# Expert-gate blocks stored whole by two transfers from two half buffers to a padded DRAM layout

## The chip, the cores and the metric

One core of one Trainium2 chip runs the whole program. The metric is the device time of one execution in microseconds (us), as the median of several runs. The engines are TensorE (PE, matmuls; PEld are its weight loads), VectorE (DVE), ScalarE (ACT), GpSimd (POOL) and SyncE (SP, whose queue issues all the DMA transfers here).

## The reference

A sequence of 2,048 tokens with 512 features passes four layers, two pairs of a Fourier layer (A) and a mixture of 256 small experts with 32 heads (B), each with a layer norm ahead and a residual:

```python
a = einsum("bsd,ed->bse", x, dft_hid_re);  b = einsum("bsd,ed->bse", x, dft_hid_im)
y = einsum("ts,bse->bte", dft_seq_re, a) - einsum("ts,bse->bte", dft_seq_im, b)   # A

q = einsum("nd,dhc->nhc", xf, w_q)                     # B: two halves of 128
s1 = einsum("nhd,ed->nhe", q[..., :dk], k1); s2 = einsum("nhd,ed->nhe", q[..., dk:], k2)
i1, i2 = top-2 of the 16 scores s1, of the 16 scores s2
cand = t1[..., :, None] + t2[..., None, :]             # 4 candidates, experts i1 * 16 + i2
top_s, top_e = the best 2 of the 4;  g = softmax(top_s)
act = gelu(einsum("nd,nhkd->nhk", xf, u[top_e]))
out = einsum("nhk,nhk,nhkd->nd", g, act, v[top_e])
```

Since there are only 256 experts, B can be computed densely: for each token a 16 x 16 matrix holds the sum over the heads of the gates g at (i1, i2); it is multiplied by gelu(x u^T), 256 values a token, and the product by v.

## The kernel before

**Tiles and stages.** The tokens form 16 tiles of 128. For each of the two layer pairs, units of 256 tokens (the last 256 tokens as two units of 128) pass through: the sequence DFT (`seq_unit`, L519: its matrix is streamed from DRAM in pieces of 256 KB, each split into a high part `ch` by ACT at L459 and a low part `cl` by DVE at L463; the sums are in PSUM tiles `acc`), then, for each tile (`token_tile`), the hidden DFT (L659), layer norm, a transpose of the normed rows (on PE at L747, or, for most tiles, by DVE at L715 with a store L719 and a reload L728 through DRAM, cast at L735 and L738), the scores (L777, L781), evacuated by ACT to `sc` (L786), and x u^T (L808). DVE then finds the top two of 16 by trees of maxima and comparisons (L861 to L916); L861 of the second rank is the last reader of `sc`. The results, as small numbers `q`, are transposed (L989) and evacuated (`qt`, L993).

**The blocks.** With `qt`, DVE makes one-hot masks of 16 x 16 x 4 (L1012, weighted at L1018) in four `lr` buffers of 2 KB a partition. 32 matmuls (L1028) multiply them. Since each treats four tokens at once, its result is a 64 x 64 block of which only the 4 diagonal parts (16 x 16 each, both of one token) are wanted: partition (j, e, t), free (g, t', f), wanted where t = t'. Two PSUM banks hold them; ACT evacuates them, one bank at a time (L1038), into `gs`. Four transfers (L1058), one for each t, take the diagonal parts out of every fourth partition in runs of 64 B to the DRAM tile `gdr`, and two transfers (L1066) bring them back in runs of 64 B, token by partition, as `gt`. DVE multiplies `gt` into the activation (L1069). The product is transposed on PE (L1100) and multiplied by v (L1119, L1123); L1134 adds the row, L1139 or L1144 stores it. For 13 tiles of the second layer pair this last part is put off: they turn the product on DVE (L1076), store it (L1091), and at the very end `off` loads and multiplies it (L591, evacuated at L597, added at L600, stored at L601) while PE waits for the last tile.

**Buffers.** `sc` has one buffer, which serves the scores of a tile and, later, `gs` of a tile. `lr` has four, for the masks and for the rows turned at L715. The last tile (`fine`) uses other memory: the masks lie in `ch` and `cl` buffers, `gs` in the tile `pth`, `gt` in a `raw` buffer.

**The order.** Every operation is put down as an `op` with an engine, an estimated time, what it comes after, a priority, the buffers it takes (`Hold`) and gives back, and, for a transfer, a `lag` until it has landed (at most eight in flight). `Plan.run` is a list scheduler over these estimates, and the program is written out in the order of its start times, so that each engine's queue is fixed by them. `behind` orders an operation behind another one's issue alone. Where the plan sees PE idle for over 1 us after the last sequence DFT, filler matmuls are put in (L1205), one for each 0.23 us of the gap less 0.4 us.

Of the kernel before, what the change touches and what calls it, by code (L numbers as in the profile page):

```python
# [8 lines left out]
F32 = mybir.dt.float32  # L9
# [7 lines left out]
P = 128  # L17
# [7 lines left out]
SP = 1  # L25
# [3 lines left out]
E = 16  # L29
# [20 lines left out]


LATE = 13
WARY = 0.8
FILL0 = 10
FIRST = 4
# [23 lines left out]
class Plan:  # L79
# [10 lines left out]
    def op(self, engine, us, fn, after=(), take=(), last=(), prio=(0, 0), lag=0.0, behind=(), shy=0.0):  # L90
        o = Op(len(self.ops), engine, us, fn, [a for a in after if a is not None], list(take), list(last), prio, lag,
               list(behind), shy)
        for h in o.last:
            h.users += 1
        self.ops.append(o)
        return o
# [67 lines left out]
def act(n):  # L164
    return 0.09 + n / 1.2e3
# [7 lines left out]
def spectral_peer_kernel(ctx: ExitStack, tc, x_in, cseq, ctile, dhid, wq, k1t, k2t, ut, vm, out):  # L173
    nc = tc.nc
# [4 lines left out]
    dram = ctx.enter_context(tc.tile_pool(name="dram", bufs=1, space=bass.MemoryType.DRAM))  # L179
# [3 lines left out]
    BUFS = {"acc": 4, "bank": 4, "raw": 4, "c": 3, "p": 1, "row": 4, "wr": 5, "wp": 2,  # L183
            "tok": 3, "sc": 1, "eq": 1, "act": 3, "q": 2, "top": 1, "qt": 1, "lr": 4, "gt": 1, "pp": 1, "gdr": 2, "xdr": 2, "late": 3, "ev": 3, "bn": 1}
    plan = Plan(BUFS)


    xh = [const.tile([P, D], F32R, name=m, bufs=b) for m, b in (("xh", LATE), ("xg", NT - LATE)) for _ in range(b)]
    xl = [const.tile([P, D], F32R, name=m, bufs=b) for m, b in (("xl", LATE), ("xm", NT - LATE)) for _ in range(b)]
    dh = const.tile([P, 2, KD, D], F32R, name="dh")  # L190
# [38 lines left out]
    def work(shape, dtype, name, pool=None):  # L229
        return work_pool().tile(shape, dtype, name=name, bufs=BUFS[pool or name])  # L230
# [7 lines left out]
    op = plan.op  # L238
# [365 lines left out]
    last = {}  # L604
# [3 lines left out]
    def token_tile(layer, n, i, t0, at):  # L608

        prio = (0, layer, at if at < len(units) - 1 else -1 - layer, i)  # L610
        late = (0, layer, at, i, 1)
        fine = prio[:3] == FINAL
# [3 lines left out]
        t = {}  # L616
# [31 lines left out]
        for cs in wide:  # L648
            hb, nc_ = Hold("bank"), cs.stop - cs.start
            for z, (k, ms) in enumerate(steps):  # L650
                def f(z=z, k=k, ms=ms, cs=cs):
# [4 lines left out]
                    for c in range(2):  # L656
# [7 lines left out]
                       take=[hb] if z == 0 else [], behind=[a_row],  # L664
                       last=[phold[layer, n]] if z == len(steps) - 1 else [], prio=prio)
# [103 lines left out]
        for hf in range(2):  # L769
# [22 lines left out]
            if fine:  # L792
                for z, k in enumerate(ks):
                    a_pe = op("PE", 2 * (k.stop - k.start) * MM512, lambda f=f_pch, hf=hf, k=k: f(hf, k), [a_th[z], a_pe],
                              take=[] if z else [hb], prio=prio)
# [211 lines left out]
        for hf in range(2):  # L1007
# [10 lines left out]
                nc.vector.tensor_mul(t["m", hf, 1], t["m", hf, 1], row_of(2, hf))  # L1018

            made.append(op("DVE", dve(1024, 2), f_w, [a], last=[hqt] if hf else [], prio=soon))  # L1020
        hgs, hbs = Hold("p" if fine else "sc"), [Hold("bank") for _ in range(2)]

        def f_blocks(hfs=(0, 1)):
            for hf in hfs:
# [6 lines left out]
        def f_gs(hf):  # L1031
            def f():
                if hf == 0 and fine:
                    gs = apool.tile([P, KD, 2, T], F32R, name="pth").rearrange("p k c t -> p (k c t)")[:, :N * 4].bitcast(F32)
                    t["gs"] = gs.rearrange("p (g t e) -> p g t e", t=4, e=E)
                elif hf == 0:
                    t["gs"] = work([P, 16, 4, E], F32, "sc")
                nc.scalar.activation(t["gs"][:, 8 * hf:8 * hf + 8], t["pg", hf].rearrange("p g e t -> p g t e"),  # L1038
                                     AF.Copy, scale=0.5 / GSCALE)
            return f  # L1040

        if fine:
            pe = [op("PE", 16 * MMG + 0.15, lambda hf=hf: f_blocks((hf,)), [made[hf]], take=hbs[hf:hf + 1],
                     last=hls[2 * hf:2 * hf + 1], prio=prio) for hf in range(2)]
        else:
            pe = [op("PE", 32 * MMG + 0.3, f_blocks, made, take=hbs, last=hls, prio=prio)] * 2
        evac = []
        for hf in range(2):
            evac.append(op("ACT", act(512), f_gs(hf), [pe[hf]] + evac, take=[] if hf else [hgs], last=hbs[hf:hf + 1], prio=prio))


        hd, hgt = Hold("gdr"), Hold("raw" if fine else "gt")
        moves = []
        for k in range(4):
            def f_out(k=k):
                if k == 0:
                    t["gdr"] = dram.tile([2, E, 4, 16, E], F32, name="gdr", bufs=BUFS["gdr"])
                nc.sync.dma_start(t["gdr"][:, :, k].rearrange("j e g f -> (j e) g f"), t["gs"][k::4, :, k, :])  # L1058
            moves.append(op("SP", 0.3, f_out, evac[1:], behind=moves[:1], take=[hd] if k == 0 else [], last=[hgs], prio=prio,
                            lag=2.4))  # L1060
        back = []
        for j in range(2):
            def f_in(j=j):
                if j == 0:
                    t["gt"] = piece((E, E)) if fine else work([P, E, E], F32, "gt")
                nc.sync.dma_start(t["gt"][j * 64:(j + 1) * 64], t["gdr"][j].rearrange("e t g f -> (t g) e f"))  # L1066
            back.append(op("SP", 0.4, f_in, moves, behind=back, take=[hgt] if j == 0 else [], last=[hd], prio=prio, lag=3.5,
                           shy=0.0 if fine else 0.5))
        a = op("DVE", dve(N), lambda: nc.vector.tensor_mul(t["act"], t["act"], t["gt"].rearrange("p e f -> p (e f)")),  # L1069
               back + [a_act], last=[] if deferred else [hgt], prio=prio)  # L1070
# [64 lines left out]
        if layer:  # L1135
            if at == len(units) - 1:
                for o in stores[-2:]:
                    o.behind.extend(back)
            stores.append(op("SP", load(256), lambda: nc.sync.dma_start(out[i * P:(i + 1) * P, :], t["row"]), [a],  # L1139
                             last=[hrow], prio=prio, lag=2.3))  # L1140
# [4 lines left out]
                       last=[] if keep else [hrow], prio=prio, lag=2.3)  # L1145
# [113 lines left out]
```

## Time and profile before

| | us |
|---|---|
| median of 3 runs (lowest, highest) | 1251.66 (1251.53, 1252.41) |
| profiled execution, whole time | 1250.42 |
| its span, first to last instruction | 1248.7 |
| PE, DVE, ACT busy | 1226.5, 1009.6, 483.2 |
| store of the blocks `gdr<-sc`: transfers, KB each, issue to landing | 124, 32, 2.2 |
| way back `gt<-gdr`: transfers, KB each, issue to landing | 62, 64, 2.8 |
| bytes moved by DMA | 148.19 MB |

The profile is one execution. Times in it count from the first instruction. An engine executes its queue in order, so an instruction that waits holds up all behind it. A line of the waits names the waiting engine, tile and source line, then what it waited for. A matmul's busy time overlaps that of the next one, so a busy PE is not yet a PE at its peak; an idle one has surely lost time. "SPq" rows are issues of transfers; the number with them is the time of the issue, and the transfer lands later.

### The profile page before, as it was taken

The numbers are of one execution on the slowest core, as the hardware profiler recorded it, in microseconds if no ns is written. First come the engines' busy times: TensorE is split into PE (matmuls) and PEld (weight loads), VectorE is DVE, ScalarE is ACT, GpSimd is POOL, SyncE is SP. The second block draws the span as 40 slices with busy tenths as digits, with TensorE's granted clock in tenths as the row PEclk, the third lists the DMA queues.
The fourth block names the chain that finished last, engine by engine and source line by source line (L and its number), as shares of the span: only waits on it lengthen the run. The fifth ranks groups of instructions, "written<-read, shape, count | busy, mean of one in ns | idle before, by whom it ended". The sixth has DMA issues, their size and how long they took to land.

```text
span 1248.7 us, 20707 instructions
## 1 busy us (share of the span) xinstructions
PE 1226.5 (98%) x7576; PEld 1015.0 (81%) x7576; DVE 1009.6 (81%) x2290; ACT 483.2 (39%) x994; POOL 44.5 (4%) x71
## 2 busy tenths in 40 slices
PE   9999999999999999999999999999999999999997
PEld 6877778777887888899878888777888888888985
DVE  8899997988988876869877458969595877969797
ACT  7522244333333333433563233333333333333543
POOL 2000000000000000000000000000000000000000
PEclk9999999999999999999999999999999999999999
DMA  7866551343434244341556232443526343353554
GB/s 239 263 197 223 179 159 35 85 89 93 99 92 105 67 100 111 76 119 58 129 135 153 93 104 54 122 101 90 139 76 144 85 110 85 102 118 94 127 169 127
DMA packets 317766, 148.19 MB, mean 119 GB/s; under 512 B 221920, under 2 KB 287968, under 8 KB 317664
## 3 DMA queue, kind: packets, MB, share of 16 engines
q1 hardware_dynamic: 317664, 146.87, 44.3%
q8 instruction: 59, 0.97, 0.3%
q14 instruction: 43, 0.35, 0.1%
HBM read 120.86 MB, written 25.95 MB: 118 GB/s over the span
## 4 chain that ended last, share of the span: by engine, by line
PE 64%; DVE 20%; issue 6%; DMA 5%; ACT 2%; SPq 2%; POOL 1%; POOLq 0%; DVEq 0%; ACTq 0%
PE acc L519 36%; PE bank L659 9%; PE bank L777 6%; PE bank L781 3%; DVE cl L463 2%; PE bank L808 2%; DVE eq L861 2%; DVE w L385 1%; DMA raw<-x2d 1%; PE bank L519 1%; DVE lr L1012 1%; PE bank L393 1%; DVE tmp L867 1%; DVE eq L885 1%; DMA gdr<-sc 1%
## 5 line engine op out<-in xcount | busy, mean ns | idle before, releaser
L519 PE MATMUL acc<-ch,xh 128*128 128x512 f32 (+1 forms) x868 | 328.7, 379 | 1.7 <-DVE ptl L548 1.7
L519 PE MATMUL acc<-cl,xh 128*128 128x512 f32 (+1 forms) x868 | 321.9, 371 | 0.0
L519 PE MATMUL acc<-ch,xl 128*128 128x512 f32 (+1 forms) x868 | 321.8, 371 | 0.0
L459 ACT CAST ch<-raw 128x512 fp32r<-128x512 f32 x256 | 158.5, 620 | 277.5 <-PE acc L519 235.3
L463 DVE TENSOR_TENSOR cl<-raw,ch 128x512 fp32r<-128x512 f32 x256 | 175.1, 686 | 49.1 <-ACT ch L459 38.4
L519 PEld LDWEIGHTS acc<-ch,xh 128*128 128x128 f32 x868 | 163.7, 189 | 29.3 <-issue 1.8
L519 PEld LDWEIGHTS acc<-cl,xh 128*128 128x128 f32 x868 | 163.6, 188 | 28.8
L519 PEld LDWEIGHTS acc<-ch,xl 128*128 128x128 f32 x868 | 163.8, 189 | 25.2
L777 PE MATMUL bank<-wh,tok 128*128 128x512 f32 x256 | 100.3, 392 | 2.4 <-ACT tok L735 2.4
L659 PE MATMUL bank<-dh,pth 128*128 128x512 f32 (+1 forms) x264 | 102.4, 390 | 0.2
L659 PE MATMUL bank<-dl,pth 128*128 128x512 f32 (+1 forms) x264 | 100.6, 383 | 0.0
L777 PE MATMUL bank<-wl,tok 128*128 128x512 f32 x256 | 99.7, 390 | 0.0
L867 DVE TENSOR_TENSOR tmp<-sc 128x512 f32<-128x512 f32 (+1 forms) x66 | 44.3, 671 | 66.9 <-ACT sc L786 66.5
L1012 DVE TENSOR_TENSOR lr<-iota,qt 128x1024 f16<-128x1024 f16 x124 | 80.5, 683 | 21.6 <-ACT qt L993 21.6
L659 PE MATMUL bank<-dh,ptl 128*128 128x512 f32 (+1 forms) x264 | 95.6, 384 | 0.0
L786 ACT COPY sc<-bank 128x512 f32<-128x512 f32 x64 | 37.1, 587 | 127.8 <-PE bank L781 83.3
L261 POOL TENSOR_TENSOR stats<-stats,half 128x1 f32<-128x1 f32 x64 | 43.2, 681 | 1160.7 <-DVE stats L258 1081.3
L861 DVE TENSOR_TENSOR eq<-sc,val 128x1024 f16<-128x1024 f32 (+1 forms) x66 | 78.6, 1190 | 1.6
L519 PE MATMUL acc<-ch,xg 128*128 128x512 f32 (+1 forms) x204 | 77.1, 378 | 0.0
L519 PE MATMUL acc<-cl,xg 128*128 128x512 f32 (+1 forms) x204 | 75.8, 372 | 0.1
L519 PE MATMUL acc<-ch,xm 128*128 128x512 f32 (+1 forms) x204 | 75.6, 371 | 0.0
L781 PE MATMUL bank<-wh,tok 128*128 128x512 f32 x256 | 68.6, 390 | 1.1 <-DVE tok L738 1.1
(166 smaller groups left out, 2045.2 us busy)
## 6 DMA issues: line engine op xcount, KB each, us to landing
raw<-in_cseq SPq DMA_DIRECT2D x224, 256.0 KB, 2.9
wr<-in_wq SPq DMA_DIRECT2D x32, 512.0 KB, 3.9
raw<-in_ctile SPq DMA_DIRECT2D x32, 256.0 KB, 2.9
xdr<-lr SPq DMA_DIRECT2D x25, 256.0 KB, 2.3
tok<-xdr SPq DMA_DIRECT2D x100, 64.0 KB, 2.6
wr<-in_x SPq DMA_DIRECT2D x16, 256.0 KB, 3.6
row<-in_x SPq DMA_DIRECT2D x16, 256.0 KB, 3.4
x2d<-row SPq DMA_DIRECT2D x16, 256.0 KB, 2.2
```

Source lines behind the costliest of these rows:

```text
L261: nc.gpsimd.tensor_tensor(st[:, 1:2], st[:, 1:2], half, op=ALU.pow)
L459: nc.scalar.copy(t[1], t[0])
L463: nc.vector.tensor_sub(t[2], t[0], as32(t[1]))
L519: nc.tensor.matmul(target(d), w[s][:, d * P:(d + 1) * P], moving(s % per, part), start=(s == 0 and k == 0 and d % blocks == 0), stop=(s == ...
L659: nc.tensor.matmul(t["y", cs.start], w[:, k, c, t0:t0 + P], r[:, c, k, cs], start=(z == 0 and c == 0 and m == 0), stop=(z == len(steps) - ...
L777: nc.tensor.matmul(t["pc", hf], t["th"][:, k, :], r[:, k, hf], start=(k == 0 and r is wh), stop=False)
L781: nc.tensor.matmul(t["pc", hf], t["tl"][:, k, :], wh[:, k, hf], start=False, stop=(k == KD - 1))
L786: nc.scalar.copy(t["sc"][:, :, hf, :], t["pc", hf].rearrange("p h e -> p e h"))
L808: nc.tensor.matmul(t["xu"], w[:, k, :], r[:, k, :], start=(m == 0), stop=(m == 3 * KD - 1))
L861: nc.vector.tensor_tensor(t["eq"][:, :, cols], flat("sc")[:, :, cols], val(rank_, cols), op=ALU.is_equal)
L867: nc.vector.tensor_max(t["tmp"][:, :, cols], flat("sc")[:, :8, cols], flat("sc")[:, 8:, cols])
L1012: nc.vector.tensor_tensor(t["m", hf, r], io2, row_of(r, hf), op=ALU.is_equal)
```

## The change

The two halves of the evacuated blocks become two tiles of their own: two `lr` buffers, or, for the last tile, the two halves of the same `pth` memory. Each half is stored whole, diagonal and rest, by one transfer from 128 partitions with runs of 256 B, right after its own evacuation. In DRAM, a block row of 64 numbers has a place of `STEP` = 80, and a partition's row starts every `ROW` = 16 x 80 - 16 numbers. By that offset of 16 the diagonal parts of the four token positions lie at equal steps, and each of the two transfers back can take them with one step of 80 over 64 partitions and one of 4 x `ROW` over the 16 values of e. The plan gets new estimates: 0.6 us and a lag of 2.7 for a store (0.3 and 2.4 before, for each of four), 0.6 and 3.2 for a transfer back (0.4 and 3.5).

```diff
+STEP = 5 * E
+ROW = 16 * STEP - E
...
-        hgs, hbs = Hold("p" if fine else "sc"), [Hold("bank") for _ in range(2)]
+        hgs, hbs = [Hold("p")] * 2 if fine else [Hold("lr"), Hold("lr")], [Hold("bank") for _ in range(2)]
...
-                    t["gs"] = gs.rearrange("p (g t e) -> p g t e", t=4, e=E)
-                elif hf == 0:
-                    t["gs"] = work([P, 16, 4, E], F32, "sc")
-                nc.scalar.activation(t["gs"][:, 8 * hf:8 * hf + 8], t["pg", hf].rearrange("p g e t -> p g t e"),
+                    gs = gs.rearrange("p (g t e) -> p g t e", t=4, e=E)
+                    t["gs", 0], t["gs", 1] = gs[:, :8], gs[:, 8:]
+                elif not fine:
+                    t["gs", hf] = work([P, 8, 4, E], F32, "lr")
+                nc.scalar.activation(t["gs", hf], t["pg", hf].rearrange("p g e t -> p g t e"),
                                      AF.Copy, scale=0.5 / GSCALE)
...
-            evac.append(op("ACT", act(512), f_gs(hf), [pe[hf]] + evac, take=[] if hf else [hgs], last=hbs[hf:hf + 1], prio=prio))
+            evac.append(op("ACT", act(512), f_gs(hf), [pe[hf]] + evac, take=[] if fine and hf else hgs[hf:hf + 1], last=hbs[hf:hf + 1], prio=prio))
...
-        for k in range(4):
-            def f_out(k=k):
-                if k == 0:
-                    t["gdr"] = dram.tile([2, E, 4, 16, E], F32, name="gdr", bufs=BUFS["gdr"])
-                nc.sync.dma_start(t["gdr"][:, :, k].rearrange("j e g f -> (j e) g f"), t["gs"][k::4, :, k, :])
-            moves.append(op("SP", 0.3, f_out, evac[1:], behind=moves[:1], take=[hd] if k == 0 else [], last=[hgs], prio=prio,
-                            lag=2.4))
+        for hf in range(2):
+            def f_out(hf=hf):
+                if hf == 0:
+                    t["gdr"] = dram.tile([2, E, 4, ROW], F32, name="gdr", bufs=BUFS["gdr"])
+                d = t["gdr"][0]
+                d = bass.AP(d.tensor, d.offset + hf * 8 * STEP, [[ROW, P], [STEP, 8], [1, 4 * E]])
+                nc.sync.dma_start(d, t["gs", hf].rearrange("p g t e -> p g (t e)"))
+            moves.append(op("SP", 0.6, f_out, evac[hf:hf + 1], behind=moves[-1:], take=[] if hf else [hd], last=[hgs[hf]], prio=prio,
+                            lag=2.7))
...
-                nc.sync.dma_start(t["gt"][j * 64:(j + 1) * 64], t["gdr"][j].rearrange("e t g f -> (t g) e f"))
-            back.append(op("SP", 0.4, f_in, moves, behind=back, take=[hgt] if j == 0 else [], last=[hd], prio=prio, lag=3.5,
+                d = t["gdr"][j]
+                d = bass.AP(d.tensor, d.offset, [[STEP, 64], [4 * ROW, E], [1, E]])
+                nc.sync.dma_start(t["gt"][j * 64:(j + 1) * 64], d)
+            back.append(op("SP", 0.6, f_in, moves, behind=back, take=[hgt] if j == 0 else [], last=[hd], prio=prio, lag=3.2,
                            shy=0.0 if fine else 0.5))
```

## The prediction

> **What bounds the kernel now.** I read the page first, then the busy time by stages (the windows view), then who waited for whom, the DMA issues, and last the timeline at the places that these named. The page's first lines:
>
> ```profile
> span 1248.7 us, 20707 instructions
> PE 1226.5 (98%) x7576; PEld 1015.0 (81%) x7576; DVE 1009.6 (81%) x2290; ACT 483.2 (39%) x994; POOL 44.5 (4%) x71
> ```
>
> TensorE (PE) is busy for 1226.5 of 1248.7 us, so all that any edit outside TensorE can win is in the 22.2 us of idle PE. The profiled execution took 1250.42 us, 1.72 more than its span; the median of the runs is 1251.66, 1.24 above that execution. I make the sum against 1250.42 and carry the difference over to the median. Where the idle PE lies (columns: stretch, its length, then busy time and instructions of each engine, clock, DMA share, GB/s):
>
> ```profile
> 228.00:600.00 372.00, 369.36 (x2225) 309.29 (x2224) 308.95 (x758) 138.34 (x299) 14.67 (x23) 1.00 0.38 93
> 600.00:690.00 90.00, 85.92 (x547) 72.67 (x547) 68.11 (x155) 44.12 (x86) 3.55 (x4) 1.00 0.52 135
> 690.00:1203.00 513.00, 508.84 (x2890) 424.41 (x2889) 386.10 (x897) 192.51 (x403) 8.61 (x16) 1.00 0.43 107
> 1203.00:1248.70 45.70, 37.78 (x232) 29.11 (x230) 35.76 (x100) 16.80 (x38) 0.92 (x1) 0.99 0.45 121
> ```
>
> Between the first gather (about 228 us) and the last unit's end, PE idles for 2.64 + 4.08 + 4.16 = 10.9 us; in the tail, where the last tile's latency counts, for 7.9 us. The rest lies ahead of the first gather, where the change has nothing to alter. Which waits have to do with the blocks that the change touches (columns: total us, times, longest):
>
> ```profile
> ACT sc L1038 <- DVE eq L861: 43.0, 17, 7.5
> ...
> ACT sc L786 <- DVE eq L861: 24.0, 4, 7.4
> ...
> DVE lr L1012 <- ACT qt L993: 21.6, 13, 3.3
> ACT sc L786 <- DMA gdr<-sc: 20.5, 6, 7.3
> ...
> DVE act L1069 <- DMA gt<-gdr: 9.0, 10, 1.7
> ```
>
> There is a single buffer named sc, and it holds in turn the scores of a tile (L786) and the evacuated blocks of a tile (L1038). So an evacuation waits until VectorE has read the next tile's scores to the end (43.0 us), and a score copy waits until the four transfers of the blocks have landed (20.5 us). These are waits of ScalarE, which is 39% busy; they cost time only where PE then waits. PE's own list:
>
> ```profile
> PE bank L777 <- ACT tok L735: 2.4, 2, 1.3
> ...
> PE bank L989 <- DVE q L956: 1.8, 3, 0.7
> ...
> PE bank L1100 <- DVE act L1069: 1.5, 1, 1.5
> PE bank L781 <- DVE tok L738: 1.1, 1, 1.1
> ...
> PE bank L808 <- ACT sc L1038: 0.8, 1, 0.8
> ```
>
> **The change part by part. Buffers.** The blocks go to two lr buffers instead of sc. The L1038 wait of 43.0 us and the L786 wait of 20.5 us lose their cause. What that is worth on PE is read at the places where the chain from the one to the other can be followed. At 304 us it is direct: the evacuation waits 7.50 us for L861, and PE's L808, which needs one of the PSUM banks that the evacuation frees, idles for 0.76 us.
>
> ```profile
> 304.55 0.60 ACT L1038 ACTIVATE sc<-bank 128x512 f32<-128x512 f32 x1 [7.50 <-DVE eq L861]
> ...
> 305.20 0.39 PE L808 MATMUL bank<-uh,tok 128*128 128x256 f32 x1 [0.76 <-ACT sc L1038]
> ```
>
> At 817 us the four stores go out, ScalarE stands still for 7.32 us until they have landed, everything behind L786 on its queue (the casts of the next DFT pieces, L735) comes late, and PE idles 1.09 us at L781:
>
> ```profile
> 817.35 2.73 SPq L1058 DMA_DIRECT2D gdr<-sc  x4
> ...
> 823.68 1.08 ACT L786 COPY sc<-bank 128x512 f32<-128x512 f32 x2 [7.32 <-DMA gdr<-sc]
> ...
> 833.84 0.50 PE L781 MATMUL bank<-wh,tok 128*128 128x512 f32 x1 [1.09 <-DVE tok L738]
> ```
>
> **The SP queue.** Four store issues become two. At 1091 us the xdr store (L719), whose data DVE had turned from 1091.12 on, stands behind the four issues until 1094.13; its reload and cast come late by as much, and PE idles 1.15 us at L777:
>
> ```profile
> 1091.12 1.43 DVE L715 STREAM_TRANSPOSE lr<-tok 128x512 f32<-128x512 f32 x2 [0.17 <-ACT tok L272]
> 1091.39 2.65 SPq L1058 DMA_DIRECT2D gdr<-sc  x4
> 1094.13 1.05 SPq L719 DMA_DIRECT2D xdr<-lr  x2
> ...
> 1103.28 0.50 PE L777 MATMUL bank<-wh,tok 128*128 128x512 f32 x1 [1.15 <-ACT tok L735]
> ```
>
> What an issue of the new kind costs (128 partitions of 8 runs) no row shows; the neighbours are the old store (32 partitions of 16 runs) and the xdr store (128 partitions of one run):
>
> ```profile
> L1058 SPq DMA_DIRECT2D gdr<-sc x124: 577/631/1760, 228.4 to 1226.6; - x124
> ...
> L719 SPq DMA_DIRECT2D xdr<-lr x25: 319/376/624, 271.8 to 1094.8; - x25
> ```
>
> I take 0.63 us, the nearer in runs (512 of them; the new one has 1,024), with 0.38 and 1.26 (twice 0.63, by runs) as ends. Two issues then hold the queue 1.26 us in place of 2.5; at the far end nothing is saved.
>
> **The transfers.** Median landings (columns: instances, KB each, us from issue to landing):
>
> ```profile
> wr<-in_wq SPq DMA_DIRECT2D x32, 512.0 KB, 3.9
> ...
> xdr<-lr SPq DMA_DIRECT2D x25, 256.0 KB, 2.3
> ...
> gdr<-sc SPq DMA_DIRECT2D x124, 32.0 KB, 2.2
> gt<-gdr SPq DMA_DIRECT2D x62, 64.0 KB, 2.8
> ```
>
> A new store moves 128 x 8 x 64 x 4 B = 256 KB in runs of 256 B. It is no faster than the 256 KB store in runs of 2 KB (2.3), and I bound it above by the 512 KB load (3.9). I take 2.9, since the 1,024 runs are as many as gt<-gdr has (2.8). Both kinds come to 2,048 runs a tile, so the packet count stays, while the bytes grow by 384 KB a tile, 12.6 MB in all; at a DMA share of 0.38 to 0.52 they find room. The Trainium skill, "DMA: Bandwidth & Descriptors", Specifications, says that transfers reach line rate only from 512 B on and that shorter ones cost a read-modify-write; the new runs, with 256 B, stay below. By that rule alone the store would lie nearer to 3.9 than to 2.3; the 2.2 us of the 64-byte store shows no such penalty at 32 KB, and no row here shows one at 256 KB. The way back keeps its 1,024 runs of 64 B a transfer. Only their spacing in DRAM changes (320 B and 20 KB steps); I leave it at 2.8, with the same ends, 2.3 and 3.9.
>
> **The end of the span** is where the latency of a gather counts in full. The last tile's:
>
> ```profile
> 1229.99 0.60 ACT L1038 ACTIVATE pth<-bank 128x512 f32<-128x512 f32 x1 [2.01 <-PE bank L1028]
> ...
> 1231.31 0.60 ACT L1038 ACTIVATE pth<-bank 128x512 f32<-128x512 f32 x1 [0.72 <-PE bank L1028]
> ...
> 1231.93 2.63 SPq L1058 DMA_DIRECT2D gdr<-pth  x4
> ...
> 1236.36 1.38 SPq L1066 DMA_DIRECT2D raw<-gdr  x2
> ...
> 1238.86 2.66 PE L1205 MATMUL acc<-dh 128*128 128x512 f32 x11
> ...
> 1240.28 0.42 DVE L1069 TENSOR_TENSOR act<-act,raw 128x256 f32<-128x256 f32 x1
> 1241.35 0.38 PE L1100 MATMUL bank<-identf,act 128*128 128x128 f32 x2
> ```
>
> Now the way back starts 1236.36 - 1231.91 = 4.45 us after the second evacuation. Afterwards the first half leaves at 1230.6, hidden by the second evacuation, and the second half needs about 3.0 us, 2.9 and 0.1 until the next issue starts: 1.4 us earlier (2.0 by the low end, 0.4 by the high one). But the multiply (L1069) is done at 1240.70, and the transpose behind it (L1100) starts at 1241.35 only, since eleven filler matmuls (L1205) stand ahead of it on PE: about 0.65 us that are lost already. Their number comes from the plan's gap. The plan's own costs take the gather from 4 x 0.3 + 2.4 + 2 x 0.4 + 3.5 = 7.9 us to 0.6 + 2.7 + 2 x 0.6 + 3.2 = 7.7 after the evacuation: 0.2 us, about one filler (2.66 us for eleven, 0.24 each). So most of the 1.4 us ends in front of the fillers, unless the PE work ahead of them also moves up: the gather of the tile before it no longer waits for sc. I take 0.5 us, nearer to the one filler, with ends 0.2 and 1.4.
>
> **The sum.** The three PE waits followed above, 0.76 + 1.09 + 1.15 = 3.0 us, and 0.5 us at the end: 3.5 us. Everything else is put at nothing: DVE and ACT run the same instructions, and PE's 1.5 + 1.8 us at L1100 and L989 I leave, since I could not follow them to the gather. 1250.42 - 3.5 = 1246.9 for a profiled execution, 1251.66 - 3.5 = **1248.2** for the median. With all five rows of PE's list gone (7.6 us) and 1.4 at the end it would be 9.0 less, 1242.7; with only 2.0 of the 3.5 had, 1249.7.
>
> **The rivals. Nothing that counts moves.** The order of every instruction is made by a list scheduler from cost estimates, and with other holds and costs it is made anew from about 228 us on. The named waits go, but PE's waits are short, scattered misjudgements of the plan, and another order has its own. For it speaks that 96.5 us of waits in the four rows with sc, gdr or gt (43.0 + 24.0 + 20.5 + 9.0) correspond to at most 7.6 us of idle PE; against it, that the most frequent cause (one buffer, two uses) is taken away rather than moved. Then only 0.5 us at the end remains: 1251.2. It reaches from 1249.2, where the forecast begins, to 1252.7, with one more wait of the size of the longest in PE's list, 1.5 us.
>
> **The new stores are slow.** If a store lands after 3.9 us, the gather is 0.4 us shorter and not 1.4, the last tile gives 0.2 us, and the SP part of the sum (1.15) shrinks to nothing, since the issues of the way back then hold that queue until the landing; 0.76 + 1.09 + 0.2 = 2.05 us remain: 1249.6. The line-rate rule above would be its reason, and a measured landing decides.
>
> **Slower: the masks wait for lr.** The four lr buffers now hold the masks (L1012 takes all four), the turned rows (L715) and, from evacuation to landing, the two halves. If the next masks or turned rows come before the halves have landed, VectorE waits in its queue, and the cl halves of the DFT pieces (L463) behind it, on which PE lives. Today L1012 waits for nothing but its own qt (21.6 us), which speaks against it, and L715 shows that a claim can follow the stores closely, which speaks for it. The price: 96.5 us of waits gave up to 7.6 us of idle PE, 0.08 us for each. If each of the 31 tiles ahead of the last waits 3 us for lr, that is 93 x 0.08 = 7.3 us, against 3.5 won: 3.8 slower, 1255.5. It turns the sign from 3.5 / 0.08 = 44 us of waits on, 1.4 us a tile.
>
> **How the numbers follow.** The forecast gets 0.50, nothing moves 0.29, slow stores 0.07, lr 0.14. A measurement of this kernel tells changes from about 0.2%, 2.5 us. The forecast lies beyond that (1249.2 and below), the next two within it, lr above: faster 0.50, same 0.36, slower 0.14. The forecast's own range is 1242.7 to 1249.2. The whole range goes from 1243.0 (nearly all waits gone) over the two middle cases up to 1253.5, where lr has begun to cost: it leaves out most of lr's 0.14 and a little at the low end.
>
> **What would show it.** Stores gdr<-lr, 62 of them, 256 KB each, landing at 2.3 to 3.3 us with an issue of about 0.63; some 12.6 MB more, the packets under 512 B hardly changed in number; no wait of the evacuation on eq L861 and none of L786 on a landing; PE idle between 228 and 1203 us down from 10.9 to 7 or 8; the last way back within 3.3 us of the last evacuation. I am wrong if PE's idle there stays at 10 or more, if a DVE wait on gdr<-lr stands among the first rows, or if the fillers ahead of the last L1100 grow by what the gather saves.

## The result

The changed kernel takes 1238.62 us (median of 4 runs, 1237.93 to 1239.08) against 1251.6 us in 4 runs of the kernel before beside them: a ratio of 0.9902, 95% interval 0.989 to 0.9914. The prediction had the sign right and the size wrong: 3.5 us were forecast, 13.0 came, and 1238.62 lies below the low end of the range. Its profiled execution took 1238.99 us. The first lines of its page:

```profile
span 1237.2 us, 20626 instructions
PE 1223.0 (99%) x7572; PEld 1015.8 (82%) x7572; DVE 1007.8 (81%) x2290; ACT 484.9 (39%) x994; POOL 45.3 (4%) x71
```

The span is 11.5 us shorter. (The medians lie 13.0 apart: the profiled execution of before was 1.2 us faster than its kernel's median, that of the changed kernel 0.4 slower.) Idle PE falls from 22.2 to 14.2 us, which is 8.0 of it. The other 3.5 us come out of PE's *busy* time: four fillers fewer (4 x 0.23 = 0.9 us), and some 2.6 us by which the same matmuls follow each other more closely.

The same stretches in the windows view:

```profile
228.00:600.00 372.00, 370.50 (x2231) 311.56 (x2230) 309.86 (x758) 139.65 (x299) 16.01 (x23) 1.00 0.43 107
600.00:690.00 90.00, 89.59 (x591) 77.55 (x590) 70.17 (x160) 47.44 (x89) 3.55 (x5) 1.00 0.57 150
690.00:1203.00 513.00, 512.01 (x2896) 427.38 (x2895) 391.39 (x914) 194.10 (x409) 8.98 (x16) 1.00 0.47 119
1203.00:1237.20 34.20, 26.49 (x178) 20.06 (x176) 26.12 (x76) 12.52 (x27) 0.00 (x0) 1.00 0.52 146
```

PE's idle time in the first three is 1.50 + 0.41 + 0.99 = 2.9 us, where it was 10.9. At the boundary of the layer pairs (600 to 690 us) 591 matmuls fit in the 90 us that held 547.

The best yardstick is the end of the last matmul of the sequence DFT, behind which only the tail is left. From the timeline of PE, before and then after:

```profile
1197.36 0.28 PE L519 MATMUL acc<-cl,xg 128*128 128x256 f32 x1
```

```profile
1186.55 0.28 PE L521 MATMUL acc<-cl,xg 128*128 128x256 f32 x1
```

It ends at 1197.64 and at 1186.83: **10.8 us** of the 11.5 were won ahead of it. The tail behind it went from 51.1 to 50.4, **0.7 us**. In the rest of this document "DFT end" is this point and "tail" what follows it.

The waits that answer to those shown of before (total us, times, longest):

```profile
ACT sc L788 <- DVE eq L863: 30.1, 7, 5.6
...
ACT lr L1041 <- PE bank L1030: 19.8, 14, 4.7
...
DVE lr L1014 <- ACT qt L995: 12.2, 10, 3.1
```

The evacuation (now L1041) waits for its own matmuls and no longer for VectorE's comparisons; its 43.0 us are gone, and so are the 20.5 us of the score copy behind the landings. The score copy's wait for the comparisons, the first row, stays (24.0 before). The masks (L1014) wait for `qt` alone, as before, and no row for `lr` buffers stands near the top. The tile that waited 7.50 us at 304 us goes like this now (timeline):

```profile
286.49 0.69 PE L1030 MATMUL bank<-lr 128*64 128x64 f16 x32
...
287.86 1.06 ACT L1041 ACTIVATE lr<-bank 128x512 f32<-128x512 f32 x2
...
288.47 1.01 SPq L1063 DMA_DIRECT2D gdr<-lr  x2
...
292.37 1.33 SPq L1073 DMA_DIRECT2D gt<-gdr  x2
...
298.18 0.42 DVE L1076 TENSOR_TENSOR act<-act,gt 128x256 f32<-128x256 f32 x1
```

The blocks are evacuated 1.4 us after their first matmul starts; in the kernel before, whose matmuls of this tile started at 292.64, that took 11.9 us, to 304.55. Over all 32 tiles the mean time from the last of these matmuls to the first evacuation fell from 6.0 to 0.0 us, and to the multiply from 17.0 to 10.75. The gather itself, from the second evacuation to the last landing of the way back, hardly changed: 8.95 to 8.07 us. So the gather was not made fast; it was let start.

The transfers (instances, KB each, us to landing), and then the issues of `gdr` (shortest, median, longest in ns):

```profile
gdr<-lr SPq DMA_DIRECT2D x62, 256.0 KB, 3.7
...
gt<-gdr SPq DMA_DIRECT2D x62, 64.0 KB, 3.0
...
gdr<-pth SPq DMA_DIRECT2D x2, 256.0 KB, 2.6
```

```profile
L1063 SPq DMA_DIRECT2D gdr<-lr x62: 366/424/1599, 221.9 to 1207.4; - x62
...
L1073 SPq DMA_DIRECT2D gt<-gdr x62: 579/640/1373, 226.7 to 1211.4; - x62
```

A store lands 0.8 us later than I took, and holds the queue for 0.42 us where I took 0.63.

### The profile page after: what moved, and what is told of

Same layout as the page of the kernel before. It is cut to its first block, busy times and chain, and to the rows that moved or that the text cites. A ratio compares the mean times of both kernels' runs of the same rounds, so it can differ in the third digit from the quotient of the medians.

```text
span 1237.2 us, 20626 instructions
## 1 busy us (share of the span) xinstructions
PE 1223.0 (99%) x7572; PEld 1015.8 (82%) x7572; DVE 1007.8 (81%) x2290; ACT 484.9 (39%) x994; POOL 45.3 (4%) x71
## 2 busy tenths in 40 slices
DMA packets 316742, 160.76 MB, mean 130 GB/s; under 512 B 220897, under 2 KB 286945, under 8 KB 316641
## 5 line engine op out<-in xcount | busy, mean ns | idle before, releaser
L1014 DVE TENSOR_TENSOR lr<-iota,qt 128x1024 f16<-128x1024 f16 x124 | 80.8, 684 | 12.3 <-ACT qt L995 12.2
```

The source lines that it names most:

```text
L1014: nc.vector.tensor_tensor(t["m", hf, r], io2, row_of(r, hf), op=ALU.is_equal)
```

## The experiments

All of them run the kernel's whole work; they differ in where the blocks lie, how they are stored, and what the plan is told. The recorded texts name three theories. A: the gain comes from the blocks leaving `sc`. B: it comes from two transfers in place of four. C: luck, the new order simply has fewer bad places. From tied_plan on, A has two forms, called D and W here. D: the single `sc` buffer costs through the *plan*: since blocks and scores can't both hold it, the scheduler puts one tile's evacuation and the next one's scores behind each other, and PE's work with them. W: the real waits on the chip cost (evacuations behind the comparisons, score copies behind the landings). Each ratio is to runs of the kernel before taken beside it. Results (DFT end, idle PE from 228 us to the DFT end, and evacuation, the mean us from the last blocks matmul to the first evacuation, are from each kernel's one profiled execution; the first half can leave before the second half's matmuls end, hence values at or below 0):

| kernel | blocks in | stores a tile | ratio (95%) | DFT end | idle | evac. |
|---|---|---|---|---|---|---|
| before | sc | 4 of 32 KB | 1 | 1197.6 | 10.9 | 6.0 |
| changed | lr | 2 of 256 KB | .9902 (.9890–.9914) | 1186.8 | 2.7 | 0.0 |
| halves_in_sc | sc | 2 of 256 KB | .9988 (.9978–.9998) | 1194.4 | 7.4 | 5.8 |
| halves_in_sc_b | sc | 2 of 256 KB | .9971 (.9955–.9988) | 1195.0 | 9.5 | 7.4 |
| halves_in_sc_c | sc | 2 of 256 KB | .9991 (.9982–1.0001) | 1195.4 | 8.0 | 5.6 |
| tied_plan | lr, plan sc | 2 of 256 KB | .9930 (.9910–.9950) | 1190.4 | 4.8 | 4.4 |
| tied_plan_b | lr, plan sc | 2 of 256 KB | .9973 (.9963–.9984) | 1193.3 | 7.4 | 6.1 |
| tied_plan_c | lr, plan sc | 2 of 256 KB | .9997 (.9987–1.0008) | 1195.5 | 9.0 | 4.0 |
| evac_waits_eq | lr, plan sc | 2 of 256 KB | .9955 (.9940–.9970) | 1189.5 | 4.8 | 5.7 |
| other_costs | lr | 2 of 256 KB | .9885 (.9869–.9901) | 1184.5 | 1.1 | 0.05 |
| other_costs_b | lr | 2 of 256 KB | .9903 (.9888–.9918) | 1185.6 | 1.9 | 0.1 |
| measured_costs | lr | 2 of 256 KB | .9917 (.9902–.9932) | 1184.2 | 0.7 | 0.05 |
| early_told | lr | 2 of 256 KB | 1.0209 (1.0192–1.0226) | 1220.2 | 23.3 | 0.0 |
| four_small | one lr of 4 KB | 4 of 32 KB | .9924 (.9909–.9938) | 1189.7 | 3.2 | 0.0 |
| two_whole | one lr of 4 KB | 2 of 256 KB | .9905 (.9888–.9921) | 1187.0 | 3.0 | −0.1 |
| eight_small | lr | 8 of 16 KB | .9962 (.9948–.9976) | 1192.8 | 6.6 | 0.1 |
| eight_whole | lr | 8 of 64 KB | .9899 (.9883–.9916) | 1186.6 | 2.3 | 0.1 |
| eight_small_told | lr | 8 of 16 KB | 1.0024 (1.0013–1.0035) | 1196.5 | 8.7 | −0.1 |
| banks_late | lr | 2 of 256 KB | .9905 (.9888–.9921) | 1188.2 | 2.7 | 0.0 |
| scores_late | lr | 2 of 256 KB | .9988 (.9978–.9997) | 1192.0 | 5.8 | −0.1 |

Single runs of one kernel lie up to some us apart (15 runs of the kernel before: 1249.45 to 1254.21), so a us more or less in the last three columns says nothing.

**One part alone: whole stores, blocks still in sc.** The edit of halves_in_sc to the changed kernel:

```diff
-        hgs, hbs = [Hold("p")] * 2 if fine else [Hold("lr"), Hold("lr")], [Hold("bank") for _ in range(2)]
+        hgs, hbs = [Hold("p" if fine else "sc")] * 2, [Hold("bank") for _ in range(2)]
...
+                    gs = work([P, 16, 4, E], F32, "sc")
+                    t["gs", 0], t["gs", 1] = gs[:, :8], gs[:, 8:]
```

The plan's estimate for a store is 0.7 us and a lag of 2.8 here, since with 0.6 and 2.7 the scheduler finds no way through.

> The changed kernel with the two evacuated halves put back into the single sc buffer (one tile of 4 KB a partition); the two whole stores, the padded layout and the transfers back stay. The plan's estimate of a store is 0.7 us and a lag of 2.8, since the plan has no solution with 0.6 and 2.7. Theory A (the gain comes from the blocks leaving the sc buffer, so that the evacuation follows its matmuls at once): 1248 to 1253 us, evacuations wait again for eq, some 6 us after the matmuls. Rival B (the gain comes from two transfers in place of four): 1238 to 1242 us. Rival C (the new order is luckier): anywhere, since the order is new again.

Ratio 0.9988 (1249.4 us), as A said: about a tenth of the gain; the granted clock has a share in that, told below. Its waits show why, and its window at the boundary that nothing improved there:

```profile
ACT sc L1042 <- DVE eq L863: 41.9, 16, 5.6
...
ACT sc L788 <- DMA gdr<-sc: 21.0, 9, 6.2
```

```profile
600.00:690.00 90.00, 86.24 (x541) 73.00 (x541) 70.45 (x160) 46.19 (x88) 3.80 (x5) 0.98 0.56 151
```

The two waits for `sc` are as long as before the change (43.0 and 20.5).

**The other part alone: two halves in lr, small stores.** eight_small is the kernel before with the two `lr` halves and, for each half, the four strided stores of before at half their size:

```diff
-        hgs, hbs = Hold("p" if fine else "sc"), [Hold("bank") for _ in range(2)]
+        hgs, hbs = [Hold("p")] * 2 if fine else [Hold("lr"), Hold("lr")], [Hold("bank") for _ in range(2)]
...
-        for k in range(4):
+        for hf, k in itertools.product(range(2), range(4)):
...
-                nc.sync.dma_start(t["gdr"][:, :, k].rearrange("j e g f -> (j e) g f"), t["gs"][k::4, :, k, :])
+                nc.sync.dma_start(t["gdr"][:, :, k, 8 * hf:8 * hf + 8].rearrange("j e g f -> (j e) g f"), t["gs", hf][k::4, :, k, :])
```

> The kernel before with the blocks in two lr halves, each stored as soon as it is evacuated, but with stores of the diagonal parts as before, 64 B a run, now four for each half, eight in all of 16 KB; layout and way back as before. Theory A: 1238 to 1243 us although SP issues twice as many stores as before, evacuations right behind the matmuls. Rival B: 1251 us or more, by up to 2.5 us a tile of issues on the queue. Rival C: anywhere.

Ratio 0.9962 (1246.4 us), outside both ranges: more than whole stores in `sc` gave, but not the whole. Whether the number of the issues or their form holds it back is the question for eight_whole below.

**Only the plan keeps the tie.** tied_plan is the changed kernel in all that runs; only the scheduler is told that an evacuation still takes `sc` and that the stores give it back (estimates as in halves_in_sc; parts of the two changed lines):

```diff
+        htie = Hold("sc")
...
-take=[] if fine and hf else hgs[hf:hf + 1],
+take=([] if fine and hf else hgs[hf:hf + 1]) + ([] if fine or hf else [htie]),
...
-last=[hgs[hf]],
+last=[hgs[hf]] + ([] if fine else [htie]),
```

> The changed kernel (store estimate 0.7 and 2.8) with its two lr halves, but the plan alone also lets the first half take sc and gives it back when both stores have landed, as before: the order is made as if the blocks lay in sc, and on the chip no buffer makes anyone wait for it. Theory A in the form that the plan's order is what costs (late evacuations hold PSUM banks, later scores): 1247 to 1253 us. Theory A in the form that the unplanned waits on the chip cost: 1239 to 1243 us. Rival B: 1239 to 1243 us.

other_costs is the changed kernel without the tie, with the same two estimates (0.7 and 2.8), another order by luck alone:

> The changed kernel with the plan's estimate of a store at 0.7 us and a lag of 2.8 in place of 0.6 and 2.7, nothing else: the control for the runs that need these estimates, and a new order of the same work. Theory A and rival B: 1237 to 1241 us. Rival C: 1243 us or more is as likely as not.

The tie in the plan turns 0.9885 into 0.9930, so D has a part. But 1242.6 us lies in the range set for W, not in that for D: tied_plan is still 0.6% faster than halves_in_sc. The two traces list the same instructions in the same order on every engine, and so do those of the two pairs that follow; in each pair the real buffer alone differs. So the pair was repeated in other orders, first with 0.6 and 3.0 for a store and 0.4 and 3.5 for the way back.

> halves_in_sc once more with other estimates in the plan (store 0.6 and 3.0, back 0.4 and 3.5), so another order of the same work. Theory A: 1247 to 1252 us again, evacuations some 6 us after the matmuls. If the order's luck decides (rival C), anything from 1237 to 1254.

> tied_plan once more with the other estimates (store 0.6 and 3.0, back 0.4 and 3.5), the partner of halves_in_sc_b (ratio 0.9971) and other_costs_b (0.9903): buffers free on the chip, order as if they were not. If the three steps found with the first estimates hold for a second order: about half way, 1240 to 1245 us. If the order's luck made them: anywhere.

> The changed kernel with those estimates (store 0.6 and 3.0, back 0.4 and 3.5): a third order of the changed kernel. Theory A: 1235 to 1241 us. Rival C: 1243 us or more would be as likely as not.

Here the times with and without the real buffer are level (0.9971 and 0.9973; tied_plan_b was not half way), and freeing the plan is worth 0.7% (0.9903, in its range). A third pair, with 1.2 and 2.4 for a store:

> halves_in_sc with a third set of estimates (store 1.2 and 2.4, back 0.4 and 3.5): 1245 to 1252 us as the other two (ratios 0.9988 and 0.9971).

> tied_plan with the same third set, against halves_in_sc_c: the same order, no buffer that makes anyone wait on the chip. If the real waits cost some 7 us, as with the first set: 1239 to 1243 us. If they cost nothing, as with the second set: within 2 us of halves_in_sc_c.

Level again (0.9991 and 0.9997). The changed kernel with these estimates and no tie was not run. In tied_plan_c no evacuation waits for a comparison and no score copy for a landing; the evacuation's own row, and PE's boundary stretch, which is still like the one before the change:

```profile
ACT lr L1042 <- PE bank L1031: 10.0, 6, 5.2
```

```profile
600.00:690.00 90.00, 86.33 (x551) 74.19 (x550) 66.48 (x152) 43.66 (x83) 4.31 (x4) 0.98 0.56 148
```

So in two of three orders, with the real waits of the blocks on `sc` gone, an order made for a shared buffer is as slow as one that has the waits. C is out as the main cause: the changed kernel in four orders (0.9885, 0.9902, 0.9903, 0.9917) stays within 0.3%, far from the 1.0% to be explained, and the tied ones lie at 0.9930 to 0.9997 (only the first one's interval reaches theirs). The 0.6% of the first pair was left; evac_waits_eq was to settle it: tied_plan with the real wait put back, by a tiny copy into an `sc` buffer ahead of the evacuation:

```diff
+                    if hf == 0:
+                        gate = work([P, 16, 4, E], F32, "sc")
+                        nc.scalar.copy(gate[:, 0, 0, :1], half)
```

> The run tied_plan (same order, same buffers) with one thing put back on the chip: ahead of a tile's first evacuation ScalarE writes one number per partition into a tile of the sc buffer, so the evacuation waits again until VectorE has read the scores in sc to the end; no store reads sc, so no score copy waits for a landing. One instruction of about 0.2 us more a tile. If the real wait of the evacuation is what cost the difference between halves_in_sc (ratio 0.9988) and tied_plan (0.993): 1248 to 1250 us. If the wait of the score copies for the landing was: 1242 to 1244 us.

0.9955 lies between the two ranges and settles little. The tiny copy waits as long as the real evacuations of halves_in_sc (41.9 us):

```profile
ACT sc L1044 <- DVE eq L863: 39.1, 16, 5.6
```

So the wait for the comparisons is not the whole 0.6%, and as the intervals of 0.9955 and 0.9930 overlap, it may be none of it. Halves_in_sc_b and halves_in_sc_c wait for the comparisons as long (42.5 and 49.6 us), but for the landings only half as long as the 21.0 us of halves_in_sc:

```profile
ACT sc L788 <- DMA gdr<-sc: 10.6, 5, 5.6
```

```profile
ACT sc L788 <- DMA gdr<-sc: 10.5, 6, 4.2
```

That points at the landings as what the first pair paid for; no run tried them alone.

**The granted clock** has a share in these ratios. In tied_plan's trace TensorE's clock stands at half once for 3.4 us, right behind 3.4 us in which PE was idle for 1.5 (windows of 3.4 us, columns as in the stretches above):

```profile
662.60:666.00 3.40, 1.91 (x38) 1.34 (x38) 3.30 (x7) 1.80 (x4) 0.00 (x0) 1.00 0.69 227
666.00:669.40 3.40, 3.40 (x10) 2.62 (x9) 0.12 (x1) 0.16 (x1) 0.00 (x0) 0.50 1.00 225
```

There a 128 x 512 matmul starts every 0.427 us, elsewhere every 0.227, so one such stretch costs about 1.7 us, in PE's busy time. Between 228 us and the DFT end the kernel before and the changed one have none; halves_in_sc and tied_plan_c have one, halves_in_sc_c and tied_plan_b two, early_told five, and ahead of each (or of two in a row) PE stood idle for 1.4 us or more of 3.4. As an estimate, take (1 - granted clock) x span off every run (one reading of 0.945 and one of 0.949 left out, since their runs are not slower by as much) and compare medians with the kernel before treated alike: halves_in_sc and its two repeats gain 3.8, 3.7 and 5.0 us, the tied plans 8.3, 5.5 and 5.0, evac_waits_eq 7.7, and other_costs, other_costs_b and measured_costs 14.0, 11.9 and 12.3. So the tie in the plan costs some 6 us by this estimate, and the real buffer 4.5, 1.8 and 0 on top; halves_in_sc and its repeats have about a third of the gain, of which the lost clock takes most away in the first and the third. Since each of these stretches follows idle time of PE, I count them with what the order costs, but that is a reading, not a test.

**The form of the transfers.** eight_whole has the plan, and so the order, of eight_small, and stores whole rows, 32 partitions at a time:

```diff
-        for hf in range(2):
+        for hf, k in itertools.product(range(2), range(4)):
...
-                d = bass.AP(d.tensor, d.offset + hf * 8 * STEP, [[ROW, P], [STEP, 8], [1, 4 * E]])
-                nc.sync.dma_start(d, t["gs", hf].rearrange("p g t e -> p g (t e)"))
+                d = bass.AP(d.tensor, d.offset + hf * 8 * STEP + 32 * k * ROW, [[ROW, 32], [STEP, 8], [1, 4 * E]])
+                nc.sync.dma_start(d, t["gs", hf][32 * k:32 * k + 32].rearrange("p g t e -> p g (t e)"))
```

> The changed kernel with each half stored by four transfers of 32 partitions (64 KB, still whole, 256 B a run) in place of one; eight issues a tile, with the estimates and so the order of eight_small (ratio 0.9962). If the eight issues on the SP queue are what keeps eight_small from the changed kernel's time: 1245 to 1248 us, as eight_small or a little slower, gather about 10 us. If the form of the runs is: 1237 to 1241 us.

0.9899 against 0.9962, as good as two stores. In the same order the issues of eight_small and then of eight_whole:

```profile
L1059 SPq DMA_DIRECT2D gdr<-lr x248: 576/612/1402, 221.0 to 1217.3; - x124
```

```profile
L1063 SPq DMA_DIRECT2D gdr<-lr x248: 303/450/1818, 221.7 to 1209.0; - x124
```

A store of rows taken from every fourth partition holds the queue 0.61 us, one of 32 whole neighbours 0.45, though it moves four times the bytes. The gather is 10.35 us against 8.84, and what stands behind these issues comes late. Waits of eight_small, then of eight_whole:

```profile
ACT tok L735 <- DMA tok<-xdr: 21.5, 12, 3.5
DVE act L1070 <- DMA gt<-gdr: 14.9, 16, 3.6
```

```profile
ACT tok L737 <- DMA tok<-xdr: 5.3, 4, 2.6
...
DVE act L1076 <- DMA gt<-gdr: 1.8, 2, 1.3
```

Is the cost that the plan does not know the length? eight_small_told tells it (0.6 us for each store and each transfer back):

> eight_small (ratio 0.9962, gather some 1.5 us longer than in eight_whole and than the plan believes) with the plan told of the length: 0.6 us for each of the eight stores and each transfer back in place of 0.3 and 0.4. The gather itself stays as long. If multiplies that come later than planned are what cost eight_small its 8 us against eight_whole: 1238 to 1241 us. If the length of the gather or the 0.61 us of each issue on the queue is: 1244 to 1248 us.

No: 1.0024 (1253.0 us, above both ranges), though the wait for `xdr` halves (to 10.2 us). That reading fell. Whether the queue's time or the longer gather costs is not separated.

**Small stores with the buffer freed, four of them.** four_small is the kernel before with its four stores, layout and estimates, its blocks in `lr`. For that, `lr` becomes two buffers of 4 KB, two masks in each; two_whole does the same to the changed kernel.

```diff
-"lr": 4,
+"lr": 2,
...
-        hgs, hbs = Hold("p" if fine else "sc"), [Hold("bank") for _ in range(2)]
+        hgs, hbs = Hold("p" if fine else "lr"), [Hold("bank") for _ in range(2)]
...
-                    t["gs"] = work([P, 16, 4, E], F32, "sc")
+                    t["gs"] = work([P, 16, 4, E], F32, "lr")
```

> The change of buffers alone with the four old stores, their layout and their estimates: the four lr buffers of 2 KB become two of 4 KB, so that the blocks of a tile fit one as a single tile (the masks of a half share one, a turned row block has one for itself), and the blocks leave sc. If leaving sc is enough: 1237 to 1242 us. If the form and the number of the stores are needed as well, as eight_small (ratio 0.9962) and eight_whole (0.9899) let one think: 1243 to 1249 us.

> The partner of four_small: the changed kernel with the same two buffers of 4 KB in place of four of 2 KB, both halves in one of them, two whole stores. 1237 to 1242 us by both theories, if the coarser buffers cost nothing; what it takes more than the changed kernel is their price.

This is the plainest split of the change. Leaving `sc` gives 0.76% (0.9924; 1241.6 us, in the range for leaving being enough) with every transfer as it was; two whole stores in place of the four bring 0.9905, some 0.2% more, with intervals that overlap. Two stretches of four_small:

```profile
228.00:600.00 372.00, 370.70 (x2229) 311.23 (x2228) 311.78 (x762) 140.70 (x301) 14.59 (x23) 1.00 0.39 94
600.00:690.00 90.00, 89.61 (x592) 77.74 (x591) 68.92 (x157) 45.63 (x86) 3.54 (x5) 1.00 0.53 139
```

PE is as full as in the changed kernel (89.59 of 90 us), at 139 GB/s in place of 150.

**What the plan is told.** early_told has the changed kernel's work with a store told at 0.3 and 1.5, a way back at 0.4 and 2.6; measured_costs has about what the profile shows (0.45 and 3.5, 0.65 and 3.0).

> The changed kernel with the plan told too little: a store 0.3 us and a lag of 1.5, a transfer back 0.4 and 2.6, so that it believes in a gather about 2 us shorter than it is. The transfers themselves stay. If unplanned lateness costs: 1243 to 1248 us. If only the length of the gather does: 1237 to 1241 us.

> The changed kernel with the plan told what the trace of the changed kernel shows: a store 0.45 us and a lag of 3.5, a transfer back 0.65 and 3.0. If unplanned lateness is what is left to win: 1235 to 1238 us. If not, or if its order has other flaws: 1237 to 1241 us, as the other three orders of the changed kernel.

Told too little, the changed kernel takes 1275.5 us, far above both ranges: 3.1% more than with its own figures and 2.1% over the kernel before. The order puts the multiply and the transpose where the gather has not come back, and now real waits reach PE; the five stretches at half clock (17 us) make up some 8.5 us of the 37. Waits of early_told:

```profile
DVE act L1076 <- DMA gt<-gdr: 43.3, 27, 4.9
...
PE bank L1107 <- DVE act L1076: 14.0, 10, 2.3
```

Telling it the truth gives 0.9917, no better than the change's own figures: that the plan takes the 3.7 us landing for 2.7 costs nothing that can be measured.

**Through what the tie costs.** In the plan, a shared `sc` makes two things late: the PSUM banks of the blocks come back late, and the next scores start late. Each was put alone into the changed kernel's plan: the banks, or the score buffer, count as taken for 6.0 us longer (only the plan, by a `delay` added when a hold comes back).

```diff
-                    self.pools[h.pool].append(h.end)
+                    self.pools[h.pool].append(h.end + h.delay)
...
+        for h in hbs:
+            h.delay = 0.0 if fine else 6.0
```

In scores_late the last two lines are `hsc.delay = 0.0 if fine else 6.0`.

> The changed kernel; in the plan alone, the two PSUM banks of a tile's blocks come back 6.0 us after their evacuation, as long as the evacuation waited on average in the kernel before (mean of 32 tiles from the last blocks matmul to the first evacuation). The chip itself waits for nothing new. If the banks that the late evacuation held are what cost: 1246 to 1251 us. If not: 1237 to 1242 us.

> The changed kernel; in the plan alone, the scores' buffer sc comes back 6.0 us after its last reader, as if the blocks lay in it for the time from evacuation to landing. If the later scores are what cost: 1244 to 1251 us. If not: 1237 to 1242 us. If neither this run nor banks_late is slow, what costs is the late evacuation and multiply themselves.

Late banks cost nothing that shows (0.9905). Late scores cost 0.86%, but only half of it where the change won: the DFT end moves from 1186.8 to 1192.0 (5.2 us), and its tail grows from 50.4 to 55.8 us with 49 fillers in place of 16; the kernel before has a tail of 51.1 and 20 fillers. So late scores can stand for about half of the 10.8 us. What the other half is stays open; the multiply, which in scores_late comes no later than in the changed kernel (10.9 and 10.75 us behind the blocks matmuls, 17.0 before), may be it, but was not tried alone.

## Why the prediction was right or wrong

**The step that failed** is the middle term of the sum: "The three PE waits followed above, 0.76 + 1.09 + 1.15 = 3.0 us", together with "Everything else is put at nothing". In its place 10.8 us were won ahead of the DFT end. I took the PE waits that I could follow to the shared buffer for all that it costs. The runs showed that nearly all the others went too. PE's own waits in the changed kernel begin like this (the first row is the start of the program, and 2.0 us before as well):

```profile
PE bank L1210 <- DVE half L214: 2.0, 1, 2.0
PE bank L1107 <- DVE act L1076: 1.1, 2, 0.8
PE bank L991 <- DVE q L958: 0.9, 2, 0.6
```

The rows of 2.4 us (L777 before), 1.1 (L781) and 0.8 (L808) are down to 0.3 or off the list, and also the 4.08 us of the boundary stretch, which no single row had connected with `sc`. A buffer that two kinds of work share shapes the scheduler's whole order: tied_plan_b and tied_plan_c, with the real waits taken out, are as slow as their partners that have them (tied_plan is 0.6% faster than its own). The list of waits doesn't tell that. Of the 10.8 us, 8.0 did stand in the trace as idle PE, but under other names: an engine that the plan itself puts later does not wait for `sc`. Through which operations the order costs is open for about half of it, as scores_late shows.

**A bound that is none.** I said that all that an edit outside TensorE can win lies in the 22.2 us of idle PE. The change won less than that, but not out of idle time alone. PE's busy time fell by 3.5 us as well, 2.6 of it without fewer instructions. The matmul records are longer (0.39 us for 128 x 512 in the groups) than the time from one start to the next when nothing disturbs them (0.227 us), so the first 0.16 us of every gap counts as busy. Take the median interval from one start to the next, form by form, for the 7,304 matmuls up to the DFT end: they need 1166.9 us in both kernels. From the first start to the last, 28.4 us more went by before and 17.6 after. Idle time shows 8.0 of these 10.8.

**The tail term was right**: 0.5 us forecast, 0.7 measured. But where the saving goes was half wrong. The last tile's rows (timeline):

```profile
1219.15 0.60 ACT L1041 ACTIVATE pth<-bank 128x512 f32<-128x512 f32 x1 [2.17 <-PE bank L1030]
1219.78 1.69 SPq L1063 DMA_DIRECT2D gdr<-pth  x2
...
1220.48 0.60 ACT L1041 ACTIVATE pth<-bank 128x512 f32<-128x512 f32 x1 [0.73 <-PE bank L1030]
...
1223.82 1.35 SPq L1073 DMA_DIRECT2D raw<-gdr  x2
...
1228.35 0.69 DVE L602 TENSOR_TENSOR xl<-xl,xg 128x512 f32<-128x512 f32 x1 [0.67 <-ACT xg L599]
...
1228.89 0.84 PE L1212 MATMUL acc<-dh 128*128 128x512 f32 x3
1228.95 0.42 DVE L1076 TENSOR_TENSOR act<-act,raw 128x256 f32<-128x256 f32 x1
...
1229.57 0.38 PE L1107 MATMUL bank<-identf,act 128*128 128x128 f32 x2
```

The way back starts 2.74 us after the second evacuation (1221.08), 1.7 earlier than before; I had 1.4. Its data land at 1227.5, but the multiply starts at 1228.95, since an L602 stands ahead of it on VectorE, which itself waits for ScalarE; before, the multiply came 0.17 us after the landing. I had named the fillers as what eats the saving. They are three in this gap now, and the transpose starts 0.2 us after the multiply. So it was VectorE's queue that ate most of it: counted from the second evacuation, the multiply starts 0.5 us earlier than before, and thanks to the fewer fillers the transpose 0.95.

**The transfers.** Bytes rose by 160.76 − 148.19 = 12.57 MB (12.6 forecast), and the packets under 512 B went from 221920 to 220897, as forecast. The issue was put too long (0.42, I took 0.63, within the ends), the landing too short: 3.7 us where I wanted 2.3 to 3.3. By the Trainium skill, "DMA: Bandwidth & Descriptors", Specifications, runs below 512 B stay short of line rate; 3.7 us is indeed nearer to the 3.9 that I set for that case, though the two stores that go out in the tail land in 2.6. The rival of the slow stores had its condition all but met and its result, 1249.6, not at all. What a faster landing would be worth, no run shows. SP's queue even stands longer for it, at the way back, before and then after:

```profile
SPq L1066 <- DMA gdr<-sc: 27.7, 31, 3.1
```

```profile
SPq L1073 <- DMA gdr<-lr: 47.7, 30, 3.9
```

That is twenty us more on that queue, yet the multiply's own wait for `gt` fell from 9.0 to 2.5 us. Whether the 1.15 us at the `xdr` store went by the shorter issues or by the new order can't be told apart.

**The other rivals.** "Nothing that counts moves" leaned on the idea that each order has its own waits; four orders of the changed kernel, all at 0.9885 to 0.9917, speak against it. "The masks wait for lr" did not happen: L1014 waits for `qt`, 12.2 us in all, less than the 21.6 before. The low end of the forecast itself, 1242.7, had counted all five of PE's rows as won, and is still 4 us above what came.

## What to carry to other kernels

When an order is planned, a buffer shared by two stages costs in the order itself: ask what the scheduler would do with one buffer more, and don't price the edit by the waits that the trace can connect with it. Test it by telling the planner a tie that does not exist. Tell a planner latencies near what the profile shows: here a landing told 1 us short was harmless, but a whole gather told at 0.3 + 1.5 + 0.8 + 2.6 = 5.2 us in place of 7.7 cost 3%. Truer figures alone are no sure gain: they won nothing in measured_costs and lost 0.6% in eight_small_told. And look at the granted clock of each run before two of them are called level.

## What the hardware showed

- The time for which an issue holds SP's queue does not follow the number of runs: 0.42 us for 128 partitions of 8 runs, 0.45 for 32 neighbouring partitions of 8 runs, 0.61 to 0.63 for 32 partitions taken at a step of four with 8 or with 16 runs of 64 B, and 0.64 for the way back.
- 256 KB in runs of 256 B landed after 3.7 us, and after 2.6 in the tail. In quarters of 64 KB they landed after 1.8 us, the 16 KB stores after 1.9. By the Trainium skill, "DMA: Bandwidth & Descriptors", Rules for kernel authors, many small transfers should become one large one. The number of the stores showed no such effect here: eight whole ones of 64 KB and two of 256 KB are level (0.9899 and 0.9902). What counted, in one and the same order, was the form: 0.9962 with strided stores and 0.9899 with whole rows.
- Stretches of 3.4 us at half the granted clock came up behind 3.4 us in which PE was busy for 0.9 to 2.0 us, as in tied_plan (1.91 us) and tied_plan_c (0.86 us). A 128 x 512 matmul then started every 0.427 us in place of 0.227.
